# q transposed by DMA for half of the batches, h in halves, and a new order: attention and gated FFN on one core

## The chip, the cores and the metric

The kernel runs on one core of a Trainium2 chip. The metric is the device time of one execution in microseconds. The engines of the core work side by side, each through a list of its own in order: PE (TensorE, matrix multiplication), DVE (VectorE), ACT (ScalarE), POOL (GpSimd, which here issues the loads) and SP (SyncE, which issues the first loads and the stores). Semaphores carry the waits between them.

## What is computed

For 8 batches of 8 heads, 576 tokens and 64 channels a head:

```python
kv  = einsum('bhsd,bhse->bhde', k, v)
o   = einsum('bhsd,bhde->bhse', q, kv)
x   = o / sqrt(mean(o*o, -1) + 1e-6) * g_norm      # heads side by side: (8, 576, 512)
h   = maximum(x @ w_in, 0)                         # (8, 576, 1024)
c   = conv_w[0]*h[s-1] + conv_w[1]*h[s] + conv_w[2]*h[s+1]
out = (h * sigmoid(c)) @ w_out                     # (8, 576, 512)
```

Inputs and output are float32; the kernel multiplies in bf16.

## The kernel before

The whole kernel is one list of tokens, `ORDER`. A token such as `hm.4.6@6` calls the small function `hm` with the arguments 4 and 6; what follows the `@` names the buffer (a PSUM bank or a slot of a ring in SBUF) that the result goes to. Each function appends a few instructions to one engine's list (a few append to two), and the list of each engine stands in the order of the tokens; no scheduler changes it. A token for one engine therefore never delays another engine but by a dependence: data that is not there, or a buffer that is not free.

Tokens (s) of a batch lie in SBUF as 64 partitions times R = 9 rows, two heads on 128 partitions. `u` is 0 or 1 (heads in two groups of four), `s` a part of the tokens, `f` one of 8 slices of 128 of the 1024 hidden channels, `m` one of 9 tiles of 128 output rows of a pair of batches `p`.

| token | engine | what it does |
|---|---|---|
| `Lq Lk Lv Li Lo` | POOL | load q, k, v of a batch, a half of w_in, w_out, cast to bf16 on the way (L327, L341, L345) |
| `kv`, `kva`/`kvd` | PE, ACT/DVE | kv of a batch in 36 matmuls a u (L382), copied to `kvb` |
| `qt`, `qa`/`qd` | PE, ACT/DVE | q transposed on PE, 36 transposes of 64x64 a u (L413), copied to `qT` (L423) |
| `ot` | PE | o = kv^T q^T of half of the tokens (L440) |
| `sq`, `on`/`oq`, `nl`, `mo` | ACT, PE, ACT, DVE | batches 0 to 3: square, sum over a head's channels, 1/sqrt, scale: gives x |
| `oc`, `ss`, `ln`, `sl`, `sp`, `mu` | ACT, PE, ACT, DVE, PE, DVE | batches 4 to 7, two at a time: copy of o, sums, one 1/sqrt for two batches (`ln.4`, `ln.6`), spread to the channels, scale: gives x |
| `hp`, `rp` | PE, ACT | batch 0: a part of h for one f (L561), relu |
| `hm`, `re` | PE, ACT | batches 1 to 7: h for one f, 8 matmuls of 288 columns into two banks (L546), one relu over 576 tokens (L552) |
| `cv`, `sc` or `ta`, `aa`, `ab`, `sg` | PE, ACT or DVE, ACT | the convolution and the sigmoid (L601) |
| `mg` | DVE | h times gate (L625) |
| `om`, `ea`/`ed`, `st` | PE, ACT/DVE, SP | output tile in 8 matmuls of 512 columns (L635), copy to SBUF (L641/L646), store |
| `fi` | PE | matmuls of zeros (L266), which keep PE at work |
| `pl ps pn pc dg pg ct af` | mostly DVE | constants |

1/sqrt and sigmoid need different tables in ACT; each change from one to the other is a table load (L215), ten in all, the first at the start.

Loads stand in POOL's list in the order in which they are issued. k and v have two slots, q three, qT five; a load or copy into a slot waits until its last reader is done. The stores stand in SP's list behind the first loads. An instruction that is issued by SP waits there for its data, and what stands behind it in SP's list waits with it.

Of the kernel before, what the change touches and what calls it, by code (L numbers as in the profile page):

```python
# [70 lines left out]
nl.1.1.0@5 mo.1.1.0 ot.1.1.1@2 sq.1.1.1@6 hp.5.1@0 rp.5.1 ta.0.1.5@1 aa.0.1.3 ab.0.1.3 hp.4.1@1 rp.4.1 oq.1.1.1@4
ot.1.0.0@6 nl.1.1.1@6 mo.1.1.1 sq.1.0.0@7 hp.4.0@0 rp.4.0 om.0.0.0.4@1 on.1.0.0@4 nl.1.0.0@7 mo.1.0.0 om.0.3.0.4@0
qt.2.0.0@4 qd.2.0.0@4 qt.2.1.0@2 sg.0.1.7 hm.1.7@6 re.1.7 sg.0.1.6 hm.1.0@4 re.1.0 ta.0.1.4 aa.0.1.2 qd.2.1.0@0
hm.1.1@6 re.1.1 ab.0.1.2 mg.0.1.3 hm.1.2@2 sg.0.1.4 sg.0.1.5 re.1.2 hm.1.3@4 re.1.3 hm.1.4@6 re.1.4 ta.1.1.0@0
ta.1.1.1 aa.1.1.0 ab.1.1.0 sg.1.1.0 sg.1.1.1 kv.2.0.2@2 kvd.2.0.2@2 mg.0.1.2 om.0.1.0.4@4 qt.3.1.0@6 ot.2.0.1@2
sq.2.0.1@0 qd.3.1.0@1 om.0.0.4.4 ed.0.0@0 om.0.3.4.4 ed.0.3@1 ta.1.1.3@1 on.2.0.1@6 om.0.1.4.4 nl.2.0.1@8 mo.2.0.1@2
ed.0.1@2 ot.2.1.1@0 sq.2.1.1@1 ot.2.1.0@6 sq.2.1.0@2 om.0.2.0.4@5 on.2.1.1@2 nl.2.1.1@9 mo.2.1.1 om.0.2.4.4 ea.0.2@3
kv.3.0.2@2 kva.3.0.2@0 on.2.1.0@4 nl.2.1.0@0 mg.1.1.0 mo.2.1.0 ot.2.0.0@0 sq.2.0.0@3 hm.1.6@2 re.1.6 on.2.0.0@4
ta.1.1.2 nl.2.0.0@1 mo.2.0.0 ot.3.1.1@6 sq.3.1.1@4 hm.1.5@2 re.1.5 qt.3.0.0@4 on.3.1.1@0 nl.3.1.1@2 hm.2.5@2 re.2.5@1
qd.3.0.0@3 ot.3.0.1@4 sq.3.0.1@5 mo.3.1.1@0 hm.2.6@0 re.2.6 ta.1.1.6@0 on.3.0.1@6 nl.3.0.1@3 ta.1.1.7 aa.1.1.3  # L80
ab.1.1.3 mo.3.0.1 hm.2.2@2 re.2.2 ot.3.0.0@0 sq.3.0.0@6 Lk.4.0.4@0 Lv.4.0.4@0 Lq.5.0.4@2 hm.2.3@6 re.2.3 ot.3.1.0@2
sq.3.1.0@7 aa.1.1.1 kv.4.0.2@4 kvd.4.0.2@1 on.3.0.0@6 nl.3.0.0@4 mo.3.0.0 on.3.1.0@4 nl.3.1.0@5 mo.3.1.0 hm.2.1@6
qt.5.0.0@4 qd.5.0.0@2 ab.1.1.1 qt.4.0.0@0 qd.4.0.0@0 sg.1.1.7 st.0.2 sg.1.1.6 Lk.5.0.4@1 Lv.5.0.4@1 mg.1.1.3
ta.1.1.4@0 ta.1.1.5 sg.1.1.3 hm.3.6@2 re.3.6 sg.1.1.2 hm.3.2@4 re.3.2 mg.1.1.1 aa.1.1.2 re.2.1 hm.2.7@0 re.2.7
ta.2.2.2@1 ab.1.1.2 hm.3.0@2 re.3.0 hm.3.1@4 re.3.1 ot.4.0.0@6 qt.5.1.0@0 oc.4.0.0@6 sq.4.0.0@0 hm.3.3@2 re.3.3
qd.5.1.0@4 ta.2.2.3 sg.1.1.5 sg.1.1.4 hm.2.0@4 re.2.0 qt.4.1.0@6 ot.4.0.1@0 sq.4.0.1@1 oc.4.0.1@7 om.0.6.0.4@2
om.0.8.0.4@3 qd.4.1.0@3 ot.4.1.0@6 oc.4.1.0@8 sq.4.1.0@2 kv.5.0.2@4 ot.4.1.1@0 sq.4.1.1@3 oc.4.1.1@9 mg.1.1.2
om.0.8.4.4 ea.0.8@4 om.0.6.4.4 ea.0.6@5 ta.2.2.0@0 ta.2.2.1 kvd.5.0.2@2 ot.5.1.0@6 sq.5.1.0@4 ot.5.0.0@4 sq.5.0.0@5
ot.5.0.1@0 sq.5.0.1@6 st.0.3 oc.5.0.1@0 oc.5.1.0@1 aa.2.2.0 ab.2.2.0 oc.5.0.0@2 st.0.6 om.0.5.0.4@3 om.0.5.4.4
ea.0.5@3 aa.2.2.1 ab.2.2.1 om.0.4.0.4@2 om.0.4.4.4 ot.5.1.1@0 sq.5.1.1@7 Lq.6.0.4@0 qt.6.0.0@6 qd.6.0.0@1 qt.6.1.0@4  # L90
qd.6.1.0@0 pn ea.0.4@1 ss.4.4.2@3 ss.5.4.2 ln.4@0 sl.4@0 oc.5.1.1@3 hm.3.5@6 re.3.5 hm.3.7@4 re.3.7 om.0.7.0.4@2
om.0.7.4.4 ed.0.7@5 sp.4.1.1.4@0 mu.4.1.1@1 sp.4.0.1.4@6 mu.4.0.1 sg.2.2.3 hm.3.4@4 re.3.4 sp.4.1.0.4@2 mu.4.1.0
hm.2.4@0 re.2.4 sp.4.0.0.4@6 mu.4.0.0 sp.5.1.1.4@4 mu.5.1.1@0 Lk.6.0.4@0 Lv.6.0.4@0 kv.6.0.2@2 kva.6.0.2@0
sp.5.0.1.4@0 mu.5.0.1 hm.4.6@6 sp.5.1.0.4@2 mu.5.1.0 sg.2.2.2 sg.2.2.1 mg.2.2.1 sp.5.0.0.4@4 mu.5.0.0 ta.2.2.4@1
# [32 lines left out]
def kernel(  # L127
# [600 lines left out]
```

## Time and profile before

| | |
|---|---|
| median of 3 runs | 182.11 us (182.07 to 182.33) |
| profiled execution | 182.22 us |
| its span in the trace | 180.1 us, so 2.1 us lie around it |
| granted clock of TensorE | 1.0 throughout |
| busy PE, DVE, ACT | 169.2, 148.4, 148.8 us |
| HBM read, written | 32.5 MB, 9.4 MB |

The profile is of one execution. A busy share is an average over the span; two engines with 82% may each be full in another part. The rows of groups give a line, an engine, an operation, the tiles written and read, the shape, the count, busy time and mean duration of one, and the idle time of the engine just before them with what ended it. Back-to-back instructions of one engine overlap a little, so the busy time over the count is smaller than the mean duration. Rows of stretches give busy times per engine, the granted clock, the share of the DMA engines and the GB/s. PEld is the load of weights, which runs beside PE.

### The profile page before, as it was taken

Reading aid. Unit: us, or ns where it says so; the run is one execution under the profiler, and the core shown is the slowest. Engines: PE = TensorE matmul, PEld = TensorE weight load, DVE = VectorE, ACT = ScalarE, POOL = GpSimd, SP = SyncE. Lnnn points to the kernel's source line nnn. Section 1 sums busy time; section 2 is a strip of 40 time slices with the busy share of each in tenths; the row PEclk is TensorE's granted clock in tenths of the full one; section 3 lists DMA queues with packets and bytes.
Section 4 is the critical chain, followed back from the end, with each engine's and each line's share of the span. In section 5 each row is a group of like instructions: output and inputs, shape, how many; then the busy total and the mean of one; then the engine's idle time right before and its main releaser. Section 6 shows DMA issues by size and latency. Waiting matters only on the chain. (4 is left out here: it accounts for less than half of the span.)

```text
span 180.1 us, 5305 instructions
## 1 busy us (share of the span) xinstructions
PE 169.2 (94%) x2243; PEld 101.5 (56%) x2259; DVE 148.4 (82%) x286; ACT 148.8 (83%) x235; POOL 20.5 (11%) x32
## 2 busy tenths in 40 slices
PE   7878997999999999999999999999999999999991
PEld 2343765577456677546567764445578754444450
DVE  3496853999867899897999999989999899999730
ACT  2377798999888999999989999999699984738830
POOL 3195104000331121030000000000000000000000
PEclk9999999999999999999999999999999999999999
DMA  5999999999999999999440000401160000441495
GB/s 165 393 310 209 208 206 208 208 208 207 208 208 257 208 207 209 207 167 226 143 161 5 0 4 0 151 28 58 64 231 0 0 0 4 175 175 66 175 337 183
DMA packets 20807, 27.80 MB, mean 154 GB/s; under 512 B 1188, under 2 KB 15280, under 8 KB 20784
## 3 DMA queue, kind: packets, MB, share of 16 engines
q0 software_dynamic: 13248, 14.50, 47.7%
q1 hardware_dynamic: 6992, 11.80, 18.2%
q10 hardware_dynamic: 544, 1.18, 1.7%
q8 instruction: 17, 0.28, 0.6%
q14 instruction: 6, 0.05, 0.1%
HBM read 32.52 MB, written 9.44 MB: 233 GB/s over the span
## 5 line engine op out<-in xcount | busy, mean ns | idle before, releaser
L635 PE MATMUL banks<-w_out_sb,h 128*128 128x512 bf16 x267 | 62.8, 379 | 0.9 <-issue 0.5
L546 PE MATMUL banks<-x,w_in_sb 128*128 128x288 bf16 x448 | 58.2, 286 | 0.4 <-ACT rs L478 0.2
L546 PEld LDWEIGHTS <-w_in_sb 128*128 128x128 bf16 x448 | 42.9, 98 | 13.3 <-issue 1.0
L601 ACT ACTIVATE taps<-taps,cw 128x576 bf16<-128x576 bf16 (+1 forms) x44 | 40.6, 958 | 6.5 <-DVE taps L595 6.4
L635 PEld LDWEIGHTS <-h 128*128 128x128 bf16 x280 | 26.3, 98 | 30.5 <-issue 1.5
L552 ACT ACTIVATE h<-banks 128x576 bf16<-128x576 f32 x56 | 34.4, 666 | 2.8 <-PE banks L546 2.2
L625 DVE TENSOR_TENSOR h<-h,taps 128x1152 bf16<-128x1152 bf16 (+1 forms) x24 | 22.8, 953 | 3.6 <-ACT taps L601 1.6
L448 ACT ACTIVATE sq<-banks 128x576 bf16<-128x576 f32 (+2 forms) x32 | 20.9, 686 | 1.8 <-PE banks L440 1.8
L590 DVE TENSOR_TENSOR taps<-taps 128x1152 bf16<-128x1152 bf16 (+1 forms) x22 | 21.5, 977 | 0.5
L595 DVE TENSOR_TENSOR taps<-taps,h 128x1152 bf16<-128x1152 bf16 (+1 forms) x22 | 21.3, 973 | 0.4
L641 ACT ACTIVATE row<-banks 128x512 f32<-128x512 f32 x27 | 15.7, 617 | 4.8 <-PE banks L635 4.1
L584 DVE TENSOR_SCALAR taps<-h,cw 128x576 bf16<-128x576 bf16 (+1 forms) x44 | 18.4, 419 | 1.4 <-ACT h L568 0.7
L489 DVE SCALAR_TENSOR_TENSOR x<-banks,cw,rs 128x576 bf16<-128x576 f32 (+2 forms) x16 | 12.9, 814 | 6.9 <-ACT rs L478 6.8
L585 DVE TENSOR_SCALAR taps<-h,cw 128x576 bf16<-128x576 bf16 (+1 forms) x44 | 18.5, 420 | 0.0
L215 ACT ACT_TABLE_LOAD x10 | 12.8, 1283 | 1.9 <-issue 1.8
L423 DVE COPY qT<-banks 128x1152 bf16<-128x1152 bf16 (+2 forms) x17 | 11.8, 702 | 1.7 <-PE banks L413 1.4
L532 DVE SCALAR_TENSOR_TENSOR x<-o,cw,banks 128x576 bf16<-128x576 f32 x16 | 12.3, 809 | 1.1 <-PE banks L526 1.1
L478 ACT ACTIVATE rs<-banks,eps_sb 128x576 f32<-128x576 f32 (+2 forms) x16 | 11.8, 746 | 1.2 <-PE banks L470 0.5
L266 PE MATMUL banks<-zero 128*128 128x512 bf16 x35 | 10.4, 426 | 1.6 <-DVE zero L245 1.2
L454 ACT ACTIVATE o<-banks 128x576 f32<-128x576 f32 x16 | 10.5, 710 | 0.0
L440 PE MATMUL banks<-qT,kvb 64*64 64x288 bf16 (+2 forms) x128 | 8.5, 297 | 1.4 <-ACT kvb L396 0.9
L327 POOL DMA_DIRECT2D k_sb<-in_k_dram x7 | 5.3, 751 | 38.1 <-PE banks L382 28.2
(80 smaller groups left out, 127.0 us busy)
## 6 DMA issues: line engine op xcount, KB each, us to landing
out_dram<-row SPq DMA_DIRECT2D x35, 256.0 KB, 2.5
q_sb<-in_q_dram POOLq DMA_DIRECT2D x7, 576.0 KB, 16.3
k_sb<-in_k_dram POOLq DMA_DIRECT2D x7, 576.0 KB, 11.6
v_sb<-in_v_dram POOLq DMA_DIRECT2D x7, 576.0 KB, 14.2
stg<-in_v_dram ACTq DMA_DIRECT2D x2, 576.0 KB, 6.4
stg<-in_k_dram SPq DMA_DIRECT2D x4, 288.0 KB, 6.9
w_in_sb<-in_moe_w_in_dram POOLq DMA_DIRECT2D x2, 512.0 KB, 11.2
w_out_sb<-in_moe_w_out_dram POOLq DMA_DIRECT2D x1, 1024.0 KB, 19.4
```

Of the source, the lines that this page charges most:

```text
L448: nc.scalar.activation(T["sq", b, u, s], T["o", b, u, s], AX.Square)
L489: nc.vector.scalar_tensor_tensor(x_part(b, u, s), T["o", b, u, s], g_sb, T["rs", b, u, s], op0=AL.mult, op1=AL.mult)
L546: nc.tensor.matmul(ps[:, s, :c1 - c0], w_in_sb[:, t, f * P:(f + 1) * P], T["x", b][:, t, c0:c1], start=(t == 0), stop=(t == NT - 1))
L552: nc.scalar.activation(h_of(b, f), T["hm", b, f][:, :, :HS].rearrange("p e (r n) -> p e n r", r=R), AX.Relu)
L584: nc.vector.tensor_scalar_mul(tap[:, 0, f % 2, :n, 8:8 + S], h[:, f], cw[:, f:f + 1])
L585: nc.vector.tensor_scalar_mul(tap[:, 1, f % 2, :n, :S], h[:, f], cw[:, 2 * NF + f:2 * NF + f + 1])
L590: nc.vector.tensor_add(tap[:, 1, :, :n, :S], tap[:, 0, :, :n, 7:7 + S], tap[:, 1, :, :n, 1:1 + S])
L595: nc.vector.tensor_add(y, y, span(b, n)[:, 2 * j:2 * j + 2])
L601: nc.scalar.activation(y, y, AX.Sigmoid, scale=cw[:, NF + f:NF + f + 1])
L625: nc.vector.tensor_mul(h, h, tap_of(b, j)[:, 1, :, :n, :S])
L635: nc.tensor.matmul(T["om", p, m], h[:, f, m * P:(m + 1) * P], w_out_sb[:, f, :], start=(f == 0), stop=(f == NF - 1))
L641: nc.scalar.activation(T["os", p, m], T["om", p, m], AX.Copy)
```

## The change

q of batches 4 to 7 is no longer transposed on PE. A new token `tq` transposes it by a DMA on the SP queue, from `q_sb` to `qT`, 128 x 1152 bf16 (288 KB) an instruction, eight in all; 8 `qt` and 8 `qd` go. The DMA transposes in blocks of 128 columns, so that the rows r of q come out two to a block, the even r on the first 64 partitions and the odd r on the last. For these batches a part `s` is therefore no longer a half of the tokens but the even rows (s = 0, 5 x 64 = 320 columns) or the odd rows (s = 1, 256 columns). `kz` takes the place of `kv` and lays kv out to fit; the odd rows need kv on the other half of the partitions, so `kx` copies `kvb` with its halves exchanged to `kvx`, by two DMAs of 32 KB on the SP queue; `ox` takes the place of `ot` and reads `kvb` for s = 0 and `kvx` for s = 1. The sums and 1/sqrt of these batches are 320 wide.

h of batches 1 to 7 comes in parts: `hs.b.f.s` (4 matmuls into one bank) and `rh.b.f.s` (a relu of that part) take the place of `hm` and `re`; for batches 1 to 3 the parts are halves of the tokens, for 4 to 7 even and odd rows. There are 112 of each in place of 56.

Both halves of w_in are loaded ahead of batch 1, w_out behind it. The order is new throughout: among the rest, all 16 `hp` stand ahead of batch 1's `qt`; there are 45 filler matmuls in place of 38, eight of them in batch 1; 22 `ea` and 13 `ed` in place of 27 and 8; 3 `kva` in place of 5; `ps` and `pl` come later.

```diff
+    TQ = {int(tok.split("@")[0].split(".")[1]) for tok in ORDER.split() if tok.startswith("tq.")}
+    GW = 320 if TQ else HS
     def cols(b, s):
         if b == 0:
             return tuple(r * D for r in RS[s])
+        if b in TQ:
+            return s * 5 * D, (5 + s * 4) * D
         return s * HS, (s + 1) * HS
...
+    def tq(b, u):
+        T["qT", b, u] = ring("qT", [P, 2, S], BF16, "qT").rearrange("p a s -> p (a s)")
+        nc.sync.dma_start_transpose(
+            out=T["qT", b, u].rearrange("p (g c) -> p g c", c=P),
+            in_=qkv["q", b][:, 2 * u:2 * u + 2, :].rearrange("p t c -> p (t c)"))
+    def kz(b, u0, n):
...
+                        nc.tensor.matmul(
+                            ps[half(tt), i, u * D:(u + 1) * D],
+                            k_sb[half(i), 2 * u + tt, r * D:(r + 1) * D],
+                            v_sb[half(i), 2 * u + tt, r * D:(r + 1) * D],
+                            start=(r == 0), stop=(r == R - 1))
+    def kx(b):
+        T["kvx", b] = ring("kvx", [P, 2, 2 * D], BF16, "kvx")
+        for i in range(2):
+            nc.sync.dma_start(out=T["kvx", b][half(i)], in_=T["kvb", b][half(1 - i)])
+    def ox(b, u, s):
+        ps = T["o", b, u, s] = bank2()[:, :, :width(b, s)]
+        qt_sb = T["qT", b, u].rearrange("p (g i c) -> p g i c", i=2, c=D)
+        kv_sb = T["kvx" if s else "kvb", b]
+        for tt in range(2):
+            c = half(tt ^ s)
+            g0 = (tt * R + s) // 2
+            for i in range(2):
+                nc.tensor.matmul(
+                    ps[half(i), tt, :].rearrange("p (g c) -> p g c", c=D),
+                    kv_sb[c, i, u * D:(u + 1) * D], qt_sb[c, g0:g0 + 5 - s, i, :],
+                    start=True, stop=True)
...
+    def hs(b, f, s):
+        c0, c1 = cols(b, s)
+        ps = T["hs", b, f, s] = bank()[:, :c1 - c0]
+        for t in range(NT):
+            nc.tensor.matmul(
+                ps, w_in_sb[:, t, f * P:(f + 1) * P], T["x", b][:, t, c0:c1],
+                start=(t == 0), stop=(t == NT - 1))
+    def rh(b, f, s):
+        ps, h = T["hs", b, f, s], h_of(b, f)
+        if b in TQ:
+            h, fr = h.rearrange("p (n r) -> p n r", r=R)[:, :, s::2], ps.rearrange("p (g n) -> p n g", n=PS)
+        else:
+            h = h[:, s * HS:(s + 1) * HS].rearrange("p (n r) -> p n r", r=R)
+            fr = ps.rearrange("p (r n) -> p n r", r=R)
+        nc.scalar.activation(h, fr, AX.Relu)
```

Of the order, the part around the places that the prediction speaks of (batches 4 and 5):

```diff
+tq.4.0@4 aa.1.1.0 ab.1.1.0 tq.4.1@0
...
+Lk.4.0.4@0 Lv.4.0.4@0 Lq.5.0.4@2 tq.5.0@3
...
+kvd.4.0.2@1 kx.4@0 mo.3.1.0 sg.1.1.3 sg.1.1.2 mg.1.1.1 Lk.5.0.4@1 Lv.5.0.4@1 Lq.6.0.4@0
+hs.2.3.0@2 hs.1.6.0@3 rh.1.6.0 rh.2.3.0 hs.2.7.1@4 ta.1.1.6@1 ta.1.1.7 aa.1.1.3 ab.1.1.3 tq.5.1@2 hs.2.2.1@5 rh.2.2.1
+tq.6.0@1 hs.3.0.1@0 rh.3.0.1 hs.3.2.1@1 rh.3.2.1 hs.3.1.1@6 rh.3.1.1 sg.1.1.5 mg.1.1.2 hs.3.4.0@7 rh.3.4.0 st.0.0
+hs.3.5.1@3 hs.3.3.1@2 rh.3.3.1 rh.2.7.1 hs.3.3.0@0 hs.3.0.0@1 rh.3.0.0 rh.3.3.0 hs.3.5.0@5 sg.1.1.6 kz.5.0.2@6
+kvd.5.0.2@2 kx.5@1 ta.2.2.0@0 hs.3.1.0@2 rh.3.1.0 sg.1.1.7 mg.1.1.3 rh.3.5.0 hs.3.7.0@4 hs.3.2.0@0 rh.3.2.0 hs.3.7.1@1
+rh.3.7.1 rh.3.7.0 ta.2.2.1 om.0.8.0.4@2 aa.2.2.0 rh.3.5.1 ox.5.0.0@6 oc.5.0.0@6 ox.4.0.0@0 ox.5.1.0@4 om.0.5.0.4@3
+ta.2.2.2@1 om.0.5.4.4 ed.0.5@4 st.0.5 sq.5.0.0@0 sq.5.1.0@1 oc.5.1.0@7 oc.4.0.0@8 sq.4.0.0@2 ta.2.2.3 om.0.8.4.4
+ed.0.8@5 Lk.6.0.4@0 Lv.6.0.4@0 Lq.7.0.4@1 ab.2.2.0 ox.5.0.1@6 sq.5.0.1@3 oc.5.0.1@9 ox.4.0.1@4 sq.4.0.1@4 om.0.6.0.4@3
+om.0.6.4.4 oc.4.0.1@0 ox.5.1.1@0 oc.5.1.1@1 sq.5.1.1@5 aa.2.2.1 ed.0.6@1 ab.2.2.1 ox.4.1.0@6 st.0.1 sq.4.1.0@6
```

167 lines of the change are left out of this document (95 added, 72 removed).

## The prediction

> **What bounds the kernel now.** I read the page's shares and slices first, then a table of stretches, then the order of single instructions around the places that the change moves, then the transfers.
>
> ```profile
> PE 169.2 (94%) x2243; PEld 101.5 (56%) x2259; DVE 148.4 (82%) x286; ACT 148.8 (83%) x235; POOL 20.5 (11%) x32
> DMA  5999999999999999999440000401160000441495
> ```
>
> TensorE is busy for 169.2 of 180.1 us, and the DMA engines are full up to slice 19, about 85 us. The average hides that other engines are full too. The stretches below are cut at the ScalarE table loads (columns: stretch, its length, then busy us of PE, PEld, DVE, ACT, POOL).
>
> ```profile
> 17.80:43.48 25.68, 23.91 (x391) 17.09 (x391) 19.40 (x46) 23.51 (x42) 2.96 (x4) 1.00 1.22 207
> 43.48:63.96 20.48, 19.88 (x412) 11.89 (x414) 16.14 (x28) 18.43 (x30) 5.92 (x8) 1.00 1.20 219
> 63.96:83.72 19.76, 19.53 (x428) 12.45 (x428) 18.81 (x31) 19.73 (x34) 2.25 (x4) 1.00 1.17 200
> 83.72:117.30 33.58, 33.26 (x448) 20.64 (x451) 32.06 (x49) 32.34 (x49) 0.00 (x0) 1.00 0.25 78
> 117.30:150.00 32.70, 32.31 (x237) 20.73 (x238) 30.57 (x48) 29.89 (x42) 0.00 (x0) 1.00 0.14 50
> 150.00:180.10 30.10, 25.90 (x127) 12.34 (x127) 21.35 (x43) 15.67 (x26) 0.00 (x0) 1.00 0.45 166
> ```
>
> PE has gaps only before 43 us. From 64 to 117 us ACT is as full as PE (19.73 of 19.76, then 32.34 of 33.58). After 117 us PE alone sets the time. So work taken from PE pays in full only if ACT and the transfers let PE come earlier at the places where it waits for them.
>
> **PE: what goes and what comes.** The prices of PE work:
>
> ```profile
> 18.02 4.08 PE L561 MATMUL banks<-x,w_in_sb 128*128 128x256 bf16 x32
> 22.03 0.80 PE L413 MATMUL banks<-ident,q_sb 64*64 64x64 bf16 x72
> 25.83 0.78 PE L382 MATMUL banks<-v_sb,k_sb 64*64 64x64 bf16 x72
> 82.08 0.32 PE L440 MATMUL banks<-qT,kvb 64*64 64x288 bf16 x4
> 174.08 1.93 PE L660 MATMUL banks<-w_out_sb,h 128*128 128x256 bf16 x16
> 98.30:104.00 5.70, 5.70 (x48) 4.54 (x48) 5.63 (x8) 5.70 (x11) 0.00 (x0) 1.00 0.00 0
> 146.24:174.84 28.60, 28.50 (x135) 13.32 (x136) 25.01 (x51) 18.31 (x30) 0.00 (x0) 1.00 0.37 138
> ```
>
> The first row is the first hp; its weight load begins 0.22 us earlier, at 17.8. The last two rows are stretches of nothing but 288-wide and nothing but 512-wide matmuls: 5.70/48 = 0.119 us and 28.60/136 = 0.210 us each (136 is the count of weight loads, one a matmul). One qt of 36 transposes is 0.40 us, kv of a batch 0.78, an ot 2 x 0.119 = 0.24 (its two row halves run two at a time).
>
> Removed: 8 qt, 8 x 0.40 = 3.2 us. Added: 7 more 512-wide fillers, 7 x 0.210 = 1.5 us (8 stand behind the first hp, where none stood, and one less ahead of it). h in halves keeps four matmuls per half and the same columns (576 per f, also as 320 and 256); kz and ox keep the counts of kv and ot. Net PE work: -1.7 us. The fillers stand in the gaps of batch 1, so they may cost from 0 to 1.5 us; I count them and let the gaps shrink by part of it.
>
> **Start.** `ps` now stands behind the first hp instead of ahead of casts:
>
> ```profile
> 8.90 1.94 DVE L310 TENSOR_TENSOR bg<-bg,ident 128x8 bf16<-128x8 bf16 x10
> 10.87 0.45 DVE L311 COPY spread<-bg 128x512 bf16<-128x512 bf16 x1
> ```
>
> 2.4 us leave DVE ahead of batch 0's casts, but the last chain, of the q columns that land last, keeps its length; bounds 0 to -1 us, I take -0.4 (hp at 17.4). w_in wholly in front delays batch 1's q, k and v by one 512-KB load, about 2.5 us at the 207 GB/s above. Its cover is all 16 hp and 4 cv, 16 x 4 x 0.119 + 24 x 0.119 = 10.5 us, ahead of batch 1's qt, where before only 8 hp stood. I cost it at nothing; without that cover it would be 2.5 us.
>
> **ACT and DVE.** 56 `re` become 112 `rh`:
>
> ```profile
> 102.92 2.36 ACT L552 ACTIVATE h<-banks 128x576 bf16<-128x576 f32 x4
> 21.05 1.80 ACT L568 ACTIVATE h<-banks 128x320 bf16<-128x320 f32 x5 [0.34 <-PE banks L561]
> L641 ACT ACTIVATE row<-banks 128x512 f32<-128x512 f32 x27 | 15.7, 617 | 4.8 <-PE banks L635 4.1 <-remote 0.3 <-ACT taps L601 0.3
> L396 ACT ACTIVATE kvb<-banks 128x256 bf16<-128x256 f32 x3 | 1.2, 389 | 0.7 <-PE banks L382 0.7
> L646 DVE COPY row<-banks 128x512 f32<-128x512 f32 x8 | 5.5, 688 | 1.5 <-PE banks L635 1.5
> L423 DVE COPY qT<-banks 128x1152 bf16<-128x1152 bf16 x14 | 10.4, 753 | 1.3 <-PE banks L413 0.9 <-PE banks L440 0.3
> ```
>
> Whole, back to back: 2.36/4 = 0.59 us; a half: 1.80/5 = 0.36, a pair 0.72. That is +0.13 x 56 = 7.3 us. Off ACT go 5 ea (15.7/27 = 0.58 each, 2.9 us), 2 kva (0.8) and 2 caa (as a kva or somewhat more, 1.0): net +2.6 us. DVE loses 8 qd (10.4/14 = 0.74, 5.9 us) and gains 5 ed (0.69, 3.4) and a few small copies (about 2): net about 0; DVE decides nothing new.
>
> Where it counts is between ln.4 and ln.6, the fourth stretch. There ACT takes 33 rh for 17 re (33 x 0.36 - 17 x 0.59 = +1.9) and one ea and one kva less (-1.0): 32.34 + 0.9 = 33.2 us of ACT. PE's share between the two falls by 2.9 us (counted from the order: 33 hs, 12 om of four matmuls and 1 kz stand there, where 17 hm, 13 om, 2 kv and 2 qt stood, with 8 o, 8 sp and 2 ss in both: 0.5 + 0.8 + 0.8 + 0.8) to about 30.4. ACT then sets that stretch. It can be ahead of PE by something when the stretch begins, so the price is between 0 and 2.7 us; I take 1.5.
>
> **The transfers, and the wait that decides.** Each `tq` moves 288 KB from SBUF to SBUF on the SP queue. The SP queue is in order, and the second half of o, `ox.b.u.1`, needs `kvx`, a copy of kvb that SP also issues. For batch 5 SP holds: tq.5.1, tq.6.0, st.0.0, then the two copies of kx.5. tq.6.0 waits for the landing of q of batch 6. So kx.5 waits for it too, and behind ox.5.0.1 on PE everything is queued. When does q of batch 6 land?
>
> ```profile
> L327 POOL DMA_DIRECT2D q_sb<-in_q_dram x1: 745/745/745, 56.2 to 56.2; - x1
> DMA to landing us min/median/max: 14.7/14.7/14.7
> ...
> 50.00:55.00 5.00, 4.91 (x105) 2.98 (x103) 3.14 (x7) 4.53 (x9) 1.49 (x2) 1.00 1.21 208
> 55.00:59.00 4.00, 4.00 (x66) 2.60 (x65) 3.44 (x8) 3.32 (x6) 0.74 (x1) 1.00 1.16 265
> 59.00:77.00 18.00, 17.38 (x407) 12.06 (x407) 16.38 (x30) 17.76 (x30) 2.76 (x4) 1.00 1.21 207
> ...
> L651 SPq DMA_DIRECT2D out_dram<-row x3: 332/360/378, 51.8 to 79.0; - x3
> DMA to landing us min/median/max: 5.5/6.5/7.3
> ...
> out_dram<-row SPq DMA_DIRECT2D x2, 128.0 KB, 2.1
> ```
>
> Now at 56.2 + 14.7 = 70.9 us, in a queue that moves 207 GB/s without a pause, so it cannot come sooner by being issued sooner. Two stores (2 x 262 KB) run between 55 and 59 us; the 265 GB/s make 1060 KB in 4 us, less 524 KB of stores 536 KB of loads, where 828 KB would have moved at 207, so the stores hold the loads back by 1.4 us. The new order has no store there: -1.4. Four transposes (tq.4.0, 4.1, 5.0, 5.1) now run ahead of it. The trace has no transposing transfer. Bounds for what one takes from the loads: as a store of its size, 1.4/2 x 295/262 = 0.8 us; as slow as a whole 576-KB load at 207 GB/s, 2.8 us. I take 1.1, near the store, which is the nearest row: +4.4. q of batch 6 lands at 73.9 (72.7 to 80.7). Three or four issues of about 0.36 us follow (+1.2; an issue of a transpose is not in the trace and may be longer), and a small SP transfer under full load lands no sooner than the 5.5 us of the stores in the last rows but one: kvx is there at 80.6 (75.8 if it landed like the 2.1 us of the two small last stores on an idle queue, up to 87.4).
>
> When does PE get to ox.5.0.1? Ahead of it, from the first hp: 43 hs and 16 hp (59 x 4 x 0.119 = 28.1), 12 groups of four om (10.1), 24 cv matmuls (2.9), 6 qt (2.4), kv and kz of five batches (3.9), 15 ot and ox and 12 on and oq (27 x 0.24 = 6.5), 8 fillers (1.7): 55.6 us. By the same prices the kernel before has 58.3 us of work between 17.8 and its row at 82.08, which took 64.3: 6.0 us of gaps. Of these the fillers replace some, so 4.5 to 6.0 remain: PE arrives at 17.4 + 55.6 + 5.0 = 78.0 (77.5 to 79.0). kvx at 80.6 then makes a wait of 2.6 us in which PE does nothing.
>
> **The sum.** Behind ox.5.0.1 are 69 hs, 58 groups of om, 13 ox, 2 kz, ss, sp and oh; behind the row at 82.08 are 36 hm, 54 groups, 9 ot, 4 qt, 2 kv and the same ss, sp and oh. The difference is 69 x 0.476 + 58 x 0.84 + 13 x 0.24 + 2 x 0.78 = 86.2 against 36 x 0.952 + 54 x 0.84 + 9 x 0.24 + 4 x 0.40 + 2 x 0.78 = 85.0, or +1.2. The remainder took 174.08 + 1.93 - 82.08 = 93.9; it becomes 95.1. PE ends at 80.6 + 95.1 + 1.5 (ACT) = 177.2 instead of 176.0: +1.2 us. The tail behind it (last copy and half-row store) is unchanged. The profiled execution took 182.22 us (span 180.1 and 2.1 around it), 0.1 above the median of 182.11. Forecast: 182.22 + 1.2 - 0.1 = 183.3 us.
>
> **Rivals.** (1) kvx is in time and the kernel gets faster: the transposes cost 0.8 us or less of load time and the small copy lands in 2 to 3 us. PE goes through at 78.0, ends at 78.0 + 95.1 = 173.1, plus 0 to 1.5 for ACT: 1.4 to 2.9 us less, 179.2 to 180.7 us. The point from which this decides is kvx landing before about 78. For it: 2.1 us landings on idle queues and the size of kx; against it: 5.5 to 7.3 us in just this stretch. The Trainium skill (Advanced Engine Details and Errata, X-Bar Transpose) holds transposes to be as fast as ordinary transfers, 350 to 400 GB/s; by that one is an estimated 0.74 to 0.84 us, which is this rival's side of the range. No run before shows it.
>
> (2) The transposes are much slower than a copy: at the 2.8 us bound kvx lands at 87.4, PE ends at about 182.5 (ACT hides in the wait), +6.5 us, 188.6. The trace can't exclude it. The Trainium skill (VectorE: DVE Perf Modes, The three transpose paths) gives 1309 ns for a 128x128 block by DMA and advises TensorE where the result may go to PSUM; nine blocks in series would be an estimated 11.8 us for a tq, which would end beyond this rival.
>
> (3) The wait only eats the saving and ACT keeps up: no change, 181.7 to 182.5.
>
> **Chances.** Forecast 0.44 (182.5 to 185), rival 1 0.36, rival 2 0.12, no change 0.08. A change of 0.2% is about what a measurement of this kernel can tell from none. Faster 0.36, same 0.08, slower 0.56. The range takes in rival 1 from 179.4 and goes to transposes of about 2.4 us: 179.4 to 187.0.
>
> **What would show it.** Right: PE idle before an L440-like ox with kvx as releaser at 78 to 81 us; DMA full up to about 95 us; a landing of SP transfers of 5 us or more before that; 112 rh of about 0.36 us; ACT full between the ln's. Wrong: no wait for kvx over 0.5 us, then PE's arrival at ox.5.0.1 and the last mg tell the gain; or a tq whose landing is over 10 us, then rival 2; or gaps elsewhere, above all in batch 1 after the hp, where the order is new.

## The result: 203.4 us, slower by 12%

The changed kernel took 203.39 us (median of 4 runs, 203.10 to 203.68), the kernel before, beside it on the same chip, 182.22 (182.07 to 182.35): a ratio of 1.116, interval 1.114 to 1.118. The forecast was 183.3 us in a range of 179.4 to 187.0. The sign was right, the size was not: 21 us instead of 1. Where the executions of a kernel below lie more than 1.5% apart, its time is the median of the fast ones (one expectation gives 196.4 us, the median of all, where the text has 194.6).

The page of the profiled execution (span, shares, slices of 5.02 us each):

```profile
span 200.9 us, 4826 instructions
PE 173.5 (86%) x1974; PEld 100.4 (50%) x1974; DVE 149.0 (74%) x288; ACT 150.3 (75%) x282; POOL 20.7 (10%) x32
PE   7999998999999970101999999999999999999991
PEclk9999999999999997555799999999999999999999
DMA  5999999999999999999181500420340000050975
```

TensorE is as busy as the kernel before in sum (173.5 against 169.2 us) and everywhere but in slices 14 to 18. There, from 75 to 94 us, it stands still almost entirely, and the clock row falls to 5. So the 21 us are one hole, not a drift. The stretches across it (columns as in the prediction) and TensorE's groups of instructions in it (start, us, then what ended the idle time ahead of them):

```profile
70.00:80.00 10.00, 4.29 (x97) 2.90 (x96) 7.37 (x12) 4.76 (x14) 2.22 (x3) 0.89 1.22 185
80.00:90.00 10.00, 0.75 (x8) 0.18 (x7) 0.00 (x0) 1.30 (x2) 0.00 (x0) 0.50 1.25 189
90.00:100.00 10.00, 5.49 (x27) 1.95 (x27) 1.48 (x4) 2.86 (x5) 0.00 (x0) 0.59 0.69 114
```

```profile
84.08 0.75 PE L499 MATMUL banks<-qT,kvb 64*64 64x320 bf16 x8 [9.17 <-DMA qT<-q_sb]
94.51 0.48 PE L499 MATMUL banks<-qT,kvb 64*64 64x320 bf16 x4 [9.68 <-DMA qT<-q_sb]
94.92 4.36 PE L720 MATMUL banks<-w_out_sb,h 128*128 128x512 bf16 x12
99.21 0.41 PE L499 MATMUL banks<-qT,kvx 64*64 64x256 bf16 x8
```

L499 is `ox`. TensorE waits twice, for qT: at ox.5.0.0 for the transposed q of tq.5.0, then at ox.5.1.0 for tq.5.1. The place that the forecast named, ox.5.0.1 with kvx, is the row at 99.21, and there nothing waits any more: kvx landed at 96.4.

Why qT is so late is told by SP's queue (start, us, instructions) and by the tile's view (ns of the issue min/median/max, first and last start; then us from issue to landing):

```profile
52.18 19.95 SPq L466 DMA_TRANSPOSE qT<-q_sb  x3
72.23 1.17 SPq L488 DMA_DIRECT2D kvx<-kvb  x2
73.50 17.18 SPq L466 DMA_TRANSPOSE qT<-q_sb  x2
90.74 0.58 SPq L736 DMA_DIRECT2D out_dram<-row  x1
91.41 1.10 SPq L488 DMA_DIRECT2D kvx<-kvb  x2
```

```profile
L466 SPq DMA_TRANSPOSE qT<-q_sb x8: 1313/3408/11700, 52.2 to 109.3; - x8
DMA to landing us min/median/max: 3.2/15.2/21.4
```

An issue that I priced at 0.36 us holds SP for up to 11.7 us: SP stands at the transposes from 52 to 72 and from 73.5 to 90.7 us. Each of the four long issues ends some 3 to 5 us before the transpose ahead of it lands (63.4 and 66.2 us, 72.1 and 75.1, 78.9 and 84.0, 90.7 and 94.5): it stands until the queue ahead of it has all but drained. Two lines below the second stretch is kx.5 (91.41), which the forecast had issued at about 75. With the loads gone the last three transposes, at 100 to 109 us, are issued in 1.3 to 1.4 us and land 3.2 to 3.5 us after their issue; the four issued at 53 to 79 us took 16 to 21 us. A third wait is in the list of waits (who waits, `<-` what ended it, then us in total, times, longest): POOL may not load q of batch 7 over q of batch 4 until tq.4.1 is through.

```profile
POOL q_sb L346 <- DMA qT<-q_sb: 9.7, 1, 9.7
```

### The profile page after: what moved, and what is told of

Same layout as the page of the kernel before. It is cut to its first block, busy times and chain, and to the rows that moved or that the text cites. A ratio compares the mean times of both kernels' runs of the same rounds, so it can differ in the third digit from the quotient of the medians.

```text
span 200.9 us, 4826 instructions
## 1 busy us (share of the span) xinstructions
PE 173.5 (86%) x1974; PEld 100.4 (50%) x1974; DVE 149.0 (74%) x288; ACT 150.3 (75%) x282; POOL 20.7 (10%) x32
## 4 chain that ended last, share of the span: by engine, by line
PE 47%; DMA 31%; ACT 8%; issue 7%; POOL 2%; DVE 2%; POOLq 0%; DVEq 0%; ACTq 0%
PE banks L720 27%; DMA k_sb<-in_k_dram 12%; PE banks L627 11%; DMA qT<-q_sb 10%; DMA v_sb<-in_v_dram 9%; ACT h L639 5%; PE banks L285 4%; ACT taps L686 2%; DVE x L598 1%; PE banks L499 1%; PE banks L478 1%; PE banks L745 1%; ACT sq L508 1%; POOL k_sb L346 1%; POOL q_sb L346 1%
## 5 line engine op out<-in xcount | busy, mean ns | idle before, releaser
L720 PE MATMUL banks<-w_out_sb,h 128*128 128x512 bf16 x280 | 65.9, 386 | 0.0
L627 PE MATMUL banks<-x,w_in_sb 128*128 128x288 bf16 (+2 forms) x448 | 60.2, 286 | 0.4 <-DVE x L598 0.2
L639 ACT ACTIVATE h<-banks 128x288 bf16<-128x288 f32 (+2 forms) x112 | 43.7, 494 | 1.5 <-PE banks L627 1.3
L731 DVE COPY row<-banks 128x512 f32<-128x512 f32 x13 | 8.8, 684 | 22.7 <-PE banks L720 22.7
L675 DVE TENSOR_TENSOR taps<-taps 128x1152 bf16<-128x1152 bf16 (+1 forms) x22 | 21.5, 978 | 0.6
L499 PE MATMUL banks<-qT,kvb 64*64 64x320 bf16 x32 | 2.5, 366 | 18.8 <-DMA qT<-q_sb 18.8
L520 ACT ACTIVATE o<-banks 128x640 f32<-128x640 f32 (+1 forms) x16 | 10.6, 671 | 9.5 <-PE banks L499 9.4
L726 ACT ACTIVATE row<-banks 128x512 f32<-128x512 f32 x22 | 12.4, 596 | 4.2 <-PE banks L720 4.0
L285 PE MATMUL banks<-zero 128*128 128x512 bf16 x45 | 13.9, 438 | 1.2 <-DVE zero L264 1.2
L598 DVE SCALAR_TENSOR_TENSOR x<-o,cw,banks 128x512 bf16<-128x512 f32 (+1 forms) x16 | 12.0, 808 | 1.0 <-PE banks L592 0.8
L499 PEld LDWEIGHTS <-kvb 64*64 64x64 bf16 x32 | 0.8, 114 | 20.5 <-DMA qT<-q_sb 10.2
## 6 DMA issues: line engine op xcount, KB each, us to landing
v_sb<-in_v_dram POOLq DMA_DIRECT2D x7, 576.0 KB, 17.7
```

The source lines that it names most:

```text
L285: nc.tensor.matmul(ps[:, :w], zero[:, :P], zero[:, :w], start=True, stop=True)
L598: nc.vector.scalar_tensor_tensor(x_part(b, u, s), T["o32", b, u, s], g_sb, T["sp", b, u, s], op0=AL.mult, op1=AL.mult)
L627: nc.tensor.matmul(ps, w_in_sb[:, t, f * P:(f + 1) * P], T["x", b][:, t, c0:c1], start=(t == 0), stop=(t == NT - 1))
L639: nc.scalar.activation(h, fr, AX.Relu)
L675: nc.vector.tensor_add(tap[:, 1, :, :n, :S], tap[:, 0, :, :n, 7:7 + S], tap[:, 1, :, :n, 1:1 + S])
L720: nc.tensor.matmul(T["om", p, m], h[:, f, m * P:(m + 1) * P], w_out_sb[:, f, :], start=(f == 0), stop=(f == NF - 1))
```

## The experiments

My theory after this reading: a transposing transfer is cheap for the loads beside it and dear for its own queue; whatever stands behind it on SP, or reads it, comes 15 to 20 us late. The rivals: that the bytes cost, whatever the kind of transfer; that the loads' delay costs; that the new order or the ReLU halves cost.

For the kernels with the changed order, the table has the start of TensorE's first matmul of ox.5.0.1, the end of TensorE's work, and the end of the last packet of the loads, all from the traces (us). Behind ox.5.0.1 the changed kernel took 196.69 - 99.21 = 97.5 us and the kernel without transfers 176.19 - 78.69 = 97.5: whatever the transfers cost the changed kernel, they cost it ahead of this point.

| kernel | time | ox.5.0.1 | PE ends | last load |
|---|---|---|---|---|
| changed kernel | 203.39 | 99.21 | 196.69 | 94.15 |
| without the eight transfers | 181.84 | 78.69 | 176.19 | 86.93 |
| plain copies in their place | 187.90 | 81.68 | 181.33 | 92.70 |
| transposes that nobody reads | 202.37 | 96.22 | 195.93 | 93.75 |
| the same, kx issued by ScalarE | 201.80 | 82.43 | 195.49 | 94.46 |
| the same, SP cleared of all else | 186.27 | 82.78 | 180.26 | 95.3 |
| copies, TensorE kept busy in the wait | 186.88 | 82.69 | 180.18 | 92.48 |

**Without the transfers.**

```diff
     def tq(b, u):
-        T["qT", b, u] = ring("qT", ...)
-        nc.sync.dma_start_transpose(out=..., in_=qkv["q", b][:, 2 * u:2 * u + 2, :]...)
+        slots.pop(0)
     def ox(b, u, s):
-        qt_sb = T["qT", b, u]...
+        qt_sb = T["qT", 3, u]...
```

> The changed kernel without the eight transfers: ox of batches 4 to 7 reads the transposed q of batch 3 instead (so q of these batches is left out). Theory 1: no wait for qT, kx.5 on an idle queue, kvx in 2 to 6 us; 178 to 182 us, the most that the new order could give if the transfers were free. Rival 2 (the order or the ReLU halves cost): above 190 us.

181.84 us, ratio to before 0.998 (0.997 to 0.999). TensorE's row of ox.5.0.1:

```profile
78.69 0.41 PE L496 MATMUL banks<-qT,kvx 64*64 64x256 bf16 x8 [0.67 <-DMA kvx<-kvb]
```

TensorE is there at 78.0 and waits 0.7 us for kvx; it has no longer gap from the first hp on. So the order, the halves, w_in and the fillers together cost about what the eight `qt` that are gone bring: with transfers that are free the change would be worth 0.3 us. Rival 2 of these runs (the order costs) is out. The hole is the transfers'.

**Plain copies of the same bytes.**

```diff
-        nc.sync.dma_start_transpose(out=T["qT", b, u].rearrange("p (g c) -> p g c", c=P), in_=...)
+        nc.sync.dma_start(out=T["qT", b, u], in_=...)
```

> The changed kernel with each of the eight transposing transfers replaced by a plain copy of the same 288 KB between the same two tiles on the same queue (so o of batches 4 to 7 is made of q that isn't transposed; nothing else is left out). Theory 1 (a transposing transfer moves 1152 packets of 256 bytes, and each of them takes the place of a load's packet of 1152 bytes: it is the packets that cost): a copy has few large packets, lands in 5 to 8 us beside the loads, and the kernel takes 181 to 186 us; what is left of a wait then stands at the second half of o of batch 5 for kvx, as forecast (2.6 us). Rival 3 (it is the bytes, or a transfer inside SBUF, whatever its kind): landings above 12 us and 195 us or more.

187.90 us, ratio 1.031 (1.029 to 1.033). The tile's view, and then, from the list of waits, the one large wait of TensorE:

```profile
L466 SPq DMA_DIRECT2D qT<-q_sb x8: 465/480/552, 52.2 to 94.0; - x8
DMA to landing us min/median/max: 2.3/6.4/8.4
```

```profile
PEld L498 <- DMA kvx<-kvb: 4.9, 1, 4.9
```

This is the kernel that I forecast. A copy is issued in 0.48 us, lands after 6.4, and TensorE waits at ox.5.0.1 for kvx. The 4.9 us are of its weight load; between matmuls it stands still for 4.4 us, from 77.3 to 81.7. The forecast had 78.0 and 80.6. So bytes alone cost 6 of the 21.5 us; the kind of transfer costs the other 15.5. The difference between the two kinds stands in the pages' rows of the hardware queue (packets, MB, share of 16 engines), first the changed kernel, then this one:

```profile
q1 hardware_dynamic: 17104, 14.42, 26.0%
```

```profile
q1 hardware_dynamic: 8784, 14.42, 21.9%
```

The same bytes in 8320 more packets. The records of single packets show how they share: from 62 to 64 us the changed kernel moved 285 load packets of 1152 bytes and 284 transposing packets of 256 bytes, one for one. By that a transpose gets 284 x 256 B in 2 us, 36 GB/s, and its 288 KB (295 thousand bytes) take 8 us as long as loads run. Two more counts fit. The copies' packets of 2304 bytes share in the same way (88 beside 82 of the loads in the us from 58, 86 beside 85 in the us from 77), and with no load beside them the transposing packets of the changed kernel pass 861 in the us from 103, six times as many. So the transpose loses its time by its share, not by the transposing. A copy cut into packets of 256 bytes, which would show the size of the packets alone, was not run.

**Transposes that nobody reads.**

```diff
     def tq(b, u):
-        T["qT", b, u] = ring("qT", ...)
-        nc.sync.dma_start_transpose(out=T["qT", b, u]..., in_=...)
+        to = ring("qX", ...)
+        nc.sync.dma_start_transpose(out=to..., in_=...)
```

> As the kernel without the transfers, but all eight are made, into tiles of their own that nobody reads, at their places on the SP queue. It tells the wait for qT from what the transfers do to others (later loads, SP held at the issue, kx behind it). If only the wait for their own data costs: 180 to 185 us. If they hold up the loads and SP: kx.5 is issued at about 90 us and kvx of batch 5 lands at about 95 us as in the changed kernel, TensorE waits at the second half of o of batch 5, and the time is 194 to 203 us. My theory expects the second, since the trace of the changed kernel has kx.5 issued at 91.4 us behind the transposes.

202.37 us, ratio 1.111 (1.109 to 1.112): not waiting for the data brings one microsecond. TensorE's wait, in the list of waits:

```profile
PEld L499 <- DMA kvx<-kvb: 18.4, 1, 18.4
```

Nearly all of it has moved to ox.5.0.1 and kvx, the place of the forecast, with seven times its length. Taking away the first late reader uncovers the second. It doesn't yet tell whether kvx is late because SP is held or because the DMA engines are.

**kx on another queue.**

```diff
-            nc.sync.dma_start(out=T["kvx", b][half(i)], ...)
+            nc.scalar.dma_start(out=T["kvx", b][half(i)], ...)
```

> As the kernel whose eight transposes nobody reads (202.4 us), but the two small copies of each kx are issued by ScalarE on its own queue, so they no longer stand behind the transposes on SP. Theory 1a (the order of SP's queue costs: SP is held at the issue of tq.5.1 and tq.6.0, and kx.5 behind them): kvx of batch 5 is there at about 80 us, the wait at the second half of o of batch 5 falls from 18 us to under 5 us, and the time to 182 to 188 us although all eight transposes are made. Rival 1b (the transposes hold up the loads and everything on the DMA engines, whatever queue it is on): kvx lands at 85 us or later and the time stays above 192 us.

201.80 us, ratio 1.107 (1.105 to 1.109). Both theories missed. kvx came in time, as 1a had it: TensorE passed ox.5.0.1 at 82.43 instead of 96.22. But the time hardly moved, as 1b had it. The waits say why (the first two are one chain), and under them the transposes' row of the tile's view:

```profile
DVE row L731 <- DMA out_dram<-row: 10.6, 1, 10.6
PE banks L565 <- DVE row L731: 9.4, 1, 9.4
DVE h L710 <- ACT taps L686: 11.5, 7, 4.0
```

```profile
L466 SPq DMA_TRANSPOSE qX<-q_sb x8: 1312/3564/8811, 52.3 to 103.4; - x8
```

The stores of finished rows stand on SP too. They could not leave behind the transposes, the ring of row buffers was full, VectorE could not empty a PSUM bank, and TensorE stood at `ss` for 9.4 us. It is a third thing behind the same queue. (The rest, some 5 us between 110 and 137 us, lies around kx.6 and kx.7, which ScalarE now issues at 114 and 121 us; the third row is VectorE waiting for ScalarE, 4.7 of its 11.5 us there.)

**SP cleared of everything else.** Against the kernel above two things change: the rows have more buffers, and kx of batches 6 and 7 is back on SP.

```diff
-            nc.scalar.dma_start(out=T["kvx", b][half(i)], ...)
+            (nc.scalar if b < 6 else nc.sync).dma_start(out=T["kvx", b][half(i)], ...)
 ORDER
-ed.0.6@1 ... ed.0.4@4 ... ed.0.7@3
+ed.0.6@6 ... ed.0.4@7 ... ed.0.7@8
```

> As the kernel whose eight transposes nobody reads, with everything else of the loaded stretch taken off SP's queue: kx of batches 4 and 5 is issued by ScalarE, and the rows of batches 0 and 1 get three more buffers, so that no row waits for a store that stands behind a transpose. All eight transposes still run beside the loads and still delay them (last load at 94 us instead of 87 us). Theory 1 (SP's queue, held for 8 to 9 us at a transpose, is what costs; the loads' own delay is hidden): 183 to 188 us, TensorE without a wait of over 2 us. Rival 1b (the loads' delay costs): TensorE waits at kz.6 or kz.7 for k and v, 192 us or more.

186.27 us, ratio 1.022 (1.021 to 1.023), as theory 1 had it. SP's queue, then the largest wait for a transpose that is left on the engines that compute and the longest wait of TensorE, then the stretch behind that wait:

```profile
52.22 33.68 SPq L465 DMA_TRANSPOSE qX<-q_sb  x5
86.00 8.83 SPq L735 DMA_DIRECT2D out_dram<-row  x3
```

```profile
ACT h L638 <- DMA qX<-q_sb: 3.2, 1, 3.2
PE banks L719 <- ACT h L638: 2.0, 1, 2.0
```

```profile
76.74:80.16 3.42, 3.42 (x19) 1.22 (x18) 3.38 (x5) 3.42 (x9) 1.08 (x2) 0.50 1.01 171
```

Five transposes hold SP for 33.7 us, and TensorE hardly minds. All eight still run, and the last load lands at 95.3, later than in the changed kernel, with no wait of TensorE for k or v behind it (in the three other kernels with transposes beside the loads it waits 0.3 to 1.0 us at kz.5 for v of batch 5). So the loads' delay costs next to nothing, and what stood behind the held queue is what cost 16 us. Of the 4.4 us that remain over the kernel without transfers, 4.1 stand ahead of ox.5.0.1 (82.78 against 78.69). ScalarE is held between the two issues of kx.5 (73.1 to 75.1 us; what ends it is the landing of tq.4.1, 75.06), TensorE waits 2.0 us for a ReLU that stands behind it, and then has half the clock for 3.4 us (the last row); the wait for kvx at ox.5.0.1 is 0.8 us.

**Keeping TensorE busy in the wait.** In the kernel with copies TensorE stood still for 4.4 us, and the kernel was slower by 6.1 us. The edit:

```diff
-... ox.5.0.1@6 ...
+... fi.21.512@1 ox.5.0.1@6 ...
```

> As the kernel with plain copies (187.9 us; TensorE waits 4.9 us for kvx of batch 5 and then has a clock of 0.6), with 21 matmuls on zeros (about 4.4 us) put into that wait, so that TensorE does not stand idle. If the lower clock is what makes the wait cost more than its length (the work behind it up to ss took 7.65 us, against 5.34 us in the kernel without transfers): 185.3 to 186.2 us and a clock of 1.00 in every slice. If that stretch is slow for another reason: 187.5 us or more.

186.88 us, ratio 1.026 (1.024 to 1.027), between the two expectations. The same 109 matmuls behind ox.5.0.1 up to `ss` (the record of some is missing), in the kernel without transfers, with copies, and with copies and fillers:

```profile
78.69:84.03 5.34, 5.34 (x109) 2.41 (x110) 5.34 (x6) 4.95 (x11) 0.00 (x0) 1.00 1.18 238
```

```profile
81.68:89.33 7.65, 7.65 (x109) 2.86 (x109) 2.38 (x3) 5.12 (x10) 0.00 (x0) 0.67 1.18 246
```

```profile
82.69:88.16 5.47, 5.26 (x107) 2.50 (x108) 2.38 (x3) 4.99 (x10) 0.00 (x0) 1.00 1.19 228
```

The clock column (the third from the end) has it: 0.67 behind 4.4 us of idling, 1.00 where TensorE multiplied zeros meanwhile. The work behind the wait is 2.2 us shorter; the 21 fillers took until 82.69, 1.0 us beyond the 81.68 at which TensorE went on without them, so the kernel got 1.0 of the 2.2.

**Transposes back on TensorE, twice.** `tq` and `kx` leave, `qt` and `qd` of batches 4 to 7 come back, `kz` and `ox` become `kv` and `ot`; the two tries differ in the places and banks of qt and qd.

```diff
-tq.4.0@4 tq.4.1@0 ... kz.4.0.2@0 ... kx.4@0 ... ox.4.0.0@0
+qt.4.0.0@6 qd.4.0.0@4 qt.4.1.0@6 qd.4.1.0@0 ... kv.4.0.2@0 ... ot.4.0.0@0
```

> The changed kernel with its eight transposes of q by DMA undone: q of batches 4 to 7 goes back to TensorE (8 qt of about 0.40 us and 8 qd of about 0.74 us on VectorE, put just ahead of their first readers), kx leaves, ox becomes ot, o and h of these batches stand in halves of tokens again. The order of the rest, h in halves everywhere, w_in in front of batch 1 and the fillers stay. Theory 1 (the wait is for the transposes by DMA, nothing else of the change costs much): 181 to 187 us, TensorE without a gap of over 1 us after 45 us, clock 1.00 throughout. Rival 2 (the order, or ReLU in halves on ScalarE, costs the 21 us): above 195 us.

> The transposes back on TensorE in the changed order once more, as in the first try (196.4 us), but each qt in banks that are free at that point and its copy earlier in VectorE's order, so that no two qt share a pair of banks back to back. If the first try lost its time to the banks and to VectorE's order: 183 to 187 us, which is the time without transfers (181.8 us) plus up to 8 times 0.40 us on TensorE. If VectorE has no room for 8 more copies of 0.74 us in this order: above 190 us.

194.6 us (ratio 1.068, 1.062 to 1.074) and 194.7 us (1.069, 1.066 to 1.072; in this one qt.5.1 takes a bank that a ReLU of batch 3 has still to read, so a slice of that h is another's). The first try lies between its two expectations, the second where VectorE was to have no room. Two stretches of the second try:

```profile
60.00:70.00 10.00, 7.89 (x195) 5.49 (x193) 6.13 (x11) 7.88 (x15) 2.23 (x3) 1.00 1.20 201
70.00:80.00 10.00, 7.84 (x189) 5.82 (x190) 7.75 (x15) 6.28 (x16) 1.63 (x2) 1.00 1.02 167
```

No engine is full, so VectorE had room, and the clock is 1.00. From 59 to 81 us TensorE waits at `qt` for banks, 1.7 us for a scale on VectorE and 1.2 us for ReLUs on ScalarE, and ScalarE's ReLUs wait 5.7 us for TensorE: each waits for the other in turn. It is not a clean undo, and how fast this order would be with well-placed transposes on TensorE stays open.

**ReLU halves alone, in the order of before.**

```diff
-hm.1.7@6 re.1.7 ...
+hs.1.7.0@6 hs.1.7.1@7 rh.1.7.0 rh.1.7.1 ...
```

> The kernel before with one thing changed: h of batches 1 to 7 is made and rectified in token halves (112 ReLUs of 128x288 at about 0.36 us in place of 56 of 128x576 at 0.59 us), in the same order. My forecast put +7.3 us on ScalarE in all and 0 to 2.7 us on the path, 1.5 taken: 182.8 to 184.9 us. Rival (ScalarE's slack and the smaller pieces, which start after half of the matmuls, hide it): 181.5 to 182.5 us. Rival (ScalarE is the bound from 64 to 117 us and all of it shows): 186 to 190 us.

183.08 us, ratio 1.005 (1.003 to 1.006): +0.9 us, inside the forecast's 0 to 2.7 and under the 1.5 taken. In the stretch between the ln's, 33.58 us before, ScalarE's busy time rose from 32.34 to 33.28 us:

```profile
83.93:118.10 34.17, 34.15 (x452) 20.83 (x451) 32.13 (x49) 33.28 (x67) 0.00 (x0) 1.00 0.24 75
```

**w_in in front alone, in the order of before.**

```diff
-Li.0.4 Lq.1.0.4@1 ... Lk.1.0.4@1 Lv.1.0.4@1 ... Li.4.4
+Li.0.4 Li.4.4 Lq.1.0.4@1 ... Lk.1.0.4@1 Lv.1.0.4@1 ...
```

> The kernel before with one thing changed: the second half of w_in is loaded right behind the first, ahead of q, k and v of batch 1. My forecast costs this at nothing where all 16 hp stand ahead of batch 1; in the order of before only 8 hp do, so here q, k and v of batch 1 come some 2.5 us later for TensorE: 182 to 185 us. If the loads of batch 1 have slack in the order of before, no change.

183.87 us, ratio 1.010 (1.007 to 1.013): +1.7 us, under the forecast's price without cover (about 2.5). TensorE's row for kv of batch 1:

```profile
27.39 0.90 PE L381 MATMUL banks<-v_sb,k_sb 64*64 64x64 bf16 x72 [1.59 <-DMA v_sb<-in_v_dram]
```

It starts at 27.39 instead of 25.83, and TensorE stays 1.6 to 1.7 us late up to its last instruction: nothing in 150 us takes such a delay back.

**DMA transposes where the queue is quiet.** The order of before, with q of batches 6 and 7 alone by DMA.

```diff
+Lq.6.0.4@0 tq.6.1@0 tq.6.0@1 ... kz.6.0.2@2 kva.6.0.2@0 kx.6@0 ... Lq.7.0.4@2 tq.7.1@2 tq.7.0@3
-Lq.6.0.4@0 qt.6.0.0@6 qd.6.0.0@1 qt.6.1.0@4 qd.6.1.0@0 ... kv.6.0.2@2 kva.6.0.2@0 ... Lq.7.0.4@2
 (hm, re, ot of batches 6 and 7 as hs, rh, ox)
```

> The order of before with DMA transposes for batches 6 and 7 alone, in even and odd tokens with kz, kx, ox and h in halves for these two; batches 4 and 5 stay on TensorE. The four transposes are issued at about 83 and 90 us, when only k and v of batch 7 are still loading and no wanted data is behind them. Theory 1 (a transposing transfer costs only where loads that are wanted or copies on SP stand behind it): they land by about 95 and 103 us, ahead of their readers at 98 and 109 us; TensorE loses 4 qt (1.6 us) and ScalarE gains 16 times 0.13 us where TensorE sets the time: 180.5 to 181.8 us, faster than before. Rival (each takes 14 to 21 us there too, or the ReLU halves eat it): 182.5 us or more, with a wait of TensorE for qT at 98 us.

183.22 us, ratio 1.006 (1.004 to 1.008). The transposes did what theory 1 said, the time did not (the tile's view, then a stretch of the kernel before and the same work in this one):

```profile
L457 SPq DMA_TRANSPOSE qT<-q_sb x4: 1408/3080/5651, 79.4 to 98.6; - x4
DMA to landing us min/median/max: 3.5/6.5/11.4
```

```profile
127.85:144.60 16.75, 16.75 (x137) 13.30 (x136) 16.08 (x23) 14.78 (x22) 0.00 (x0) 1.00 0.22 79
127.75:145.24 17.49, 17.03 (x137) 13.24 (x136) 15.92 (x22) 15.93 (x35) 0.00 (x0) 1.00 0.21 76
```

They land in time: no `ox` waits for them. The first pair of qt that is gone would bring TensorE 0.7 us ahead of the kernel before at ss.4; it waits 0.4 us there for a copy on ScalarE. The second brings it 0.8 us ahead at 106.6 us, and at 109.2, behind a wait of 0.4 us for a ReLU, 0.1 is left. From 127.75 us on, over the h of batches 6 and 7, TensorE needs 17.49 us where it needed 16.75, while ScalarE's work rises from 14.78 to 15.93 us. So 1.6 us taken from a TensorE that is 94% busy bring nothing here: the waits that end the lead are for ScalarE, and where the halves stand the same work takes 0.7 us longer. That the halves are the whole of this 0.7 was not tested apart.

**Only `ps` moved.**

```diff
-... kva.0.0.1@0 ps cad.v.2.0 ...
+... mg.0.1.1 ps kv.1.0.2@0 ...
```

> The kernel before with one thing changed: the eleven small VectorE operations of ps (2.4 us) leave the casts of batch 0 and stand behind the first convolution's merge, where VectorE was idle for 2.6 us. My forecast gave the start 0.4 us, with bounds of 0 and 1. If the casts set the first hp and nothing behind it waits for loads: hp at 17.3 to 17.5 us and 181.7 to 182.0 us. If the columns of q that land last set it, or k and v of batch 1 set what follows: 182.1 to 182.4 us, the same.

181.55 us (12 runs), ratio 0.997 (0.996 to 0.998): faster than both kernels, and a little faster than the first expectation. TensorE's row of the first hp, 18.02 before:

```profile
17.31 4.08 PE L560 MATMUL banks<-x,w_in_sb 128*128 128x256 bf16 x32
```

0.71 us earlier; TensorE ends at 175.30 instead of 176.01, 0.71 earlier. An early lead is kept whole, as an early delay was.

## Why the prediction was wrong

**The step that failed** is the price of a `tq`. I asked what it takes from the loads, bounded that by 0.8 and 2.8 us, and took 1.1. That number was about right. The last load came 5.8 us later with seven copies beside it (92.70 against 86.93, 0.8 us each) and 6.8 us later with five transposes (93.75, 1.4 each): both within the bounds, on either side of 1.1. What was wrong is what I made of it: I let the transfer itself be as short as what it takes from the others. A store of the nearest rows is issued in 0.36 us and lands in 5.5 to 7.3; behind another transpose and beside loads a transpose held SP for 5 to 12 us in the changed kernel and landed after 16 to 21. The text said that the issue "may be longer" and gave it no upper bound; that bound was the term that decided.

**The wait.** Its place is right for transfers as short as I took them, as the copies show (4.9 us at ox.5.0.1 for kvx), and for transposes that nobody reads (18.4 us); its size, 2.6, is wrong for both, and in the changed kernel TensorE has already stood still twice before it gets there. So the right sign is in part luck: the waits that made the kernel slower are not the one forecast. I followed only what stands behind tq.6.0 (kx.5) and asked of no other tq when it lands; the two waits that the trace shows, for tq.5.0 and tq.5.1, I never worked out, nor POOL's load of q of batch 7 or the stores of rows behind the same queue. q of batch 6 landed at 74.8; the forecast had 73.9. It was ready in time: SP was not.

**The sum, had the price been right.** With copies, which take even less from the loads (0.8 us each) than I took for a `tq`, the kernel took 187.90 us, still above the range. TensorE ended at 181.3 instead of 177.2: 1.1 us because kvx came at 81.6 instead of 80.6, 2.2 us for the clock behind the wait, which the forecast put at nothing, and 0.9 us in the remainder.

**Rival 2** (slow transposes) came nearest. Its bound, a whole load's 2.8 us, was again of what the loads lose, not of how long SP is held, and so it stopped at 188.6. Its mark, a landing of over 10 us, is what the trace shows. The Trainium skill (VectorE: DVE Perf Modes, The three transpose paths) led to an estimate of 11.8 us for a tq; in a row beside the loads the runs show about 9 us for each (landings at 66.2, 75.1 and 84.0 us), on a quiet queue 3.3. **Rival 1** rested on short transfers; with none at all the kernel took 181.84 us, above its 179.2 to 180.7. The Trainium skill (Advanced Engine Details and Errata, X-Bar Transpose) has transposes as fast as ordinary transfers; here the copy landed after 6.4 us where the transpose took up to 21 beside the same loads, and after 2.4 where it took 3.3 on a quiet queue; the measurement decides.

**TensorE's work and the remainder.** Arrival at ox.5.0.1: forecast 78.0, measured 78.0 without transfers and 77.3 with copies (end of the group ahead of it). Remainder: forecast 95.1 + 1.5 = 96.6, measured 97.5. Both were good to a microsecond.

**The smaller terms.** ReLU halves: 1.5 taken, 0.9 measured by themselves. Start: -0.4 taken; the first hp began 0.75 us earlier (17.27 against 18.02; 17.1 to 17.7 in the other kernels of this order), and `ps` alone, in the order of before, makes 0.71. w_in: costed at nothing with its cover and "about 2.5" without; without it 1.7. The cover was not tested by itself; the kernel without transfers has no gap of TensorE over 0.5 us in batch 1.

**The clock** stood nowhere in the forecast. In the kernel with copies a wait of 4.4 us cost 2.2 us more behind it. The Trainium skill (TensorE: Matmul & The Clock Gate, Part 1) halves the clock after one idle window or more of some 3.4 us, and the 0.50 in the hole of the changed kernel agrees. By that figure a wait of 2.6 us, as forecast, is too short. The runs differ, and they decide: with SP cleared a wait of 2.0 us was followed by 3.4 us at 0.50, and so were waits of 2.1 and 2.4 us with kx issued by ScalarE, while waits of 2.1 and 3.3 us in the two tries with transposes on TensorE were not. So the forecast's wait could have cost up to half of 3.4 us more.

## What to carry to other kernels

Price a transfer twice: what it takes from the traffic beside it, and how long it holds its own queue, and for the second ask how many packets it makes, and not only how many bytes. Before a slow transfer goes on a queue, list everything behind it (copies, stores, the loads that wait for its source to come free): here three of them came out one after the other, and with the first one or two taken away the kernel got only 1.0 and 1.6 of the 21.5 us. In this kernel, whose engines are all 80 to 95% full, 1.6 us of work taken from the busiest one were worth nothing as long as the next one was not relieved too, while 0.7 us at the very start were kept to the end.

## What the runs showed of the hardware

- A transposing transfer of 288 KB from SBUF to SBUF is issued in 1.3 us and lands in 3.3 on an idle queue. Beside software-queue loads its 256-byte packets pass one for one with their 1152-byte packets (284 and 285 in 2 us, 36 GB/s), and the issue of one behind another mostly holds SP for 8.5 to 9.9 us (4.9 to 11.7 in all the runs), while each takes only about 1.4 us from the loads (a plain copy of the same bytes about 0.8).
- TensorE that idled for 4.4 us was granted a clock of 0.67 over the next 7.65 us; the same matmuls take 5.34 us at full clock. Matmuls on zeros in the wait kept it at 1.00. In the hole of the changed kernel the clock went down to 0.50. Waits of 2.0 to 2.4 us were followed by 3.4 us at 0.50 three times, and one of 3.3 us was not.
